# Attention and a maxout layer on one core: where AV, masks and loads of the first batch stand

## The chip, the core and the metric

The kernel runs on one core of a Trainium2 chip. A core has five engines that run their own instruction streams and wait for each other by semaphores: PE (matrix multiply, with PEld for its weight loads), DVE (vector), ACT (scalar functions), POOL (GpSimd) and SP (which only issues transfers here). SP's transfers of q and k and the outputs are queue q1 of the profile, POOL's transfers, which also change fp32 to bf16 on the way, are queue q0. The metric is the device time of one execution in microseconds.

## The reference

There are 8 batches of 8 heads, 576 tokens, head size 64. Attention is causal by blocks of 64 tokens; its output goes, token by token, through a layer of two products and a maximum.

```python
scores = scale * np.matmul(q, k.transpose(0, 1, 3, 2))
mask = block_i >= block_j                     # block = 64 tokens
scores = np.where(mask, scores, -1000000000.0)
scores = scores - np.max(scores, axis=-1, keepdims=True)
attn = np.exp(scores)
attn = attn / (np.sum(attn, axis=-1, keepdims=True) + 1e-09)
attn_out = np.matmul(attn, v)
x = attn_out.transpose(0, 2, 1, 3).reshape(B * S, H * D)
g = np.maximum(x @ w1, x @ w2)
out = g @ w_out
```

## The kernel before

**The algebra.** max(x w1, x w2) is max(x (w1 - w2), 0) + x w2. So the kernel forms d = w1 - w2 on DVE (`diff_w`), M = w2 w_out on PE, and then out = relu(x d) w_out + x M. M needs w2 transposed: `bT_unit` transposes a quarter of w2 (8 transposes), `m_unit` makes an eighth of M (8 matmuls). `h_unit` makes one of 8 slices of relu(x d) for 512 tokens (4 matmuls), `y_unit` 128 rows of the output (12 matmuls).

**Pairs and groups.** Heads are worked on in pairs: pair p holds two heads in the two halves of the partitions, four pairs are a batch, and two pairs are a group, whose q (and whose k) comes in one transfer of 576 KB. There are 16 groups. For each group q and k are cast to bf16, transposed on PE (`transposes`, L362) and copied to qT and kT (L370). Scores are made with keys as rows, ACT takes their exp into aT (L405), and the part of a diagonal block that a query may not see is set to zero (`mask`, L410). `av` (L496) multiplies aT with v, whose extra column of ones gives the softmax sum, and DVE divides (L502, L503). `x_out` transposes the result to xT (L534 to L540); when the last group of a batch is through, its tokens are free for h and y.

**Batch 0 in bursts.** For pairs 0 to 3 the scores of a pair are packed in four pieces, `burst_p` (queries below 256), `burst_q1`, `burst_q2` and `burst_q3`, with one exp each (768, 1024, 1024 and 384 columns over both heads). The pieces go through two PSUM buffers (`ps_s`), so a burst waits for the exp two bursts before it; some have one or two warm-up matmuls ahead of them (L416). AV of a pair is called in two parts: `av(p, [0, 1])` for queries below 256, which needs only the first piece, its masks and two of the five parts of v (6 matmuls), and `av(p, [2, 3, 4])` for the rest (24 matmuls). Everything else on PE takes turns in four PSUM buffers (`ps_m`).

**The order.** No scheduler moves anything: each engine works in the order in which the Python code calls its instructions. `fill(n)` puts n matmuls' worth of the units above in a place, taken from a fixed list whose head is four `bT_unit`s (2 each in this count) and eight `m_unit`s (4 each). POOL's order is also the gate for loads: `load_qk(g, ..., gated=True)` has POOL write one column of the target, and SP's transfer waits for that; v, w1, w2 and w_out are issued by POOL itself. A transfer that POOL issues also waits until the eighth transfer before it, which has the same semaphore, is through. From group 2 on, scores go in regions of 1024-column tiles (`tile_0` to `tile_2`); the loop over groups from the fourth on is the same in both kernels.

**Where v comes in.** v of a batch comes in five parts of 128 tokens (the last of 64), in pieces of 64 elements per head and token. Those of batch 1 are requested behind w1 and group 3: three of them at once, two behind the copies of kz (L388), which wait for kT of group 2.

Of the kernel before, what the change touches and what calls it, by code (L numbers as in the profile page):

```python
# [14 lines left out]
def kernel(  # L15
# [10 lines left out]
    nc = tc.nc  # L26
# [27 lines left out]
    NCH = 5  # L54
# [50 lines left out]
    dve, pool, act = nc.vector.tensor_copy, nc.gpsimd.tensor_copy, nc.scalar.copy  # L105

    def load_qk(g, queues, gated=False):
        b, u = divmod(g, GPB)
        for nm, src, queue in (("q", q, queues[0]), ("k", k, queues[1])):
            if queue is None or by_dma(nm, g):  # L110
                continue
            raws[nm, g] = t = raw.tile([P, 2, RPP * D], FP32, name=f"{nm}raw")
            if gated:
                nc.gpsimd.memset(t[:, 0, :1], 0.0)
            queue.dma_start(
                out=t[:],
                in_=src[b, 4 * u:4 * u + 4].rearrange(
                    "(s h) (p t) d -> (h p) s (t d)", h=2, t=RPP),
            )
# [27 lines left out]
    def cast(nm, g, parts):  # L147
        if by_dma(nm, g):
            return
        t = raws[nm, g].rearrange("p s (t d) -> p t s d", d=D)  # L150
        if (nm, g) not in qk_n:
            qk_n[nm, g] = qkn.tile([P, RPP, 2, D], BF16, name=f"{nm}n")
        n = qk_n[nm, g]
        for copy, j0, j1 in parts:
            copy(out=n[:, j0:j1], in_=t[:, j0:j1])  # L155
# [19 lines left out]
    def load_w1(j):  # L175
        w1_raw[j] = wraw.tile([P, NDM, WB], FP32, name="w1raw")
        nc.gpsimd.dma_start(out=w1_raw[j][:], in_=w1r[:, :, j * WB:(j + 1) * WB])
# [14 lines left out]
    dve, pool, act = nc.vector.tensor_copy, nc.gpsimd.tensor_copy, nc.scalar.copy  # L192
    SP, ACT = nc.sync, nc.scalar
# [138 lines left out]
    def fill(n):  # L332
        while n > 0:
            if not current:
                k = next((k for k, t in enumerate(todo) if t[2] <= done_tokens[0]), None)
                if k is None:
                    return max(0, n)
                current.append(todo.pop(k))
            t = current[0]
            next(t[1])  # L340
            n -= t[3]
            t[0] -= 1
            if not t[0]:
                current.pop()
        return 0
# [76 lines left out]
    def burst_p(p, warm=0):  # L422
        burst(p, ((0, 0, QCUT), (1, P, QCUT - P)), 0, warm)

    def burst_q1(p, warm=0):
        burst(p, ((0, QCUT, 320), (1, QCUT, 192)), 384, warm)

    def burst_q2(p, warm=0):
        burst(p, ((1, 448, P), (2, QCUT, 320), (4, 512, BLK)), 896, warm)

    def burst_q3(p, warm=0):
        burst(p, ((3, 384, 192),), 1408, warm)

    def masks_p(p, eng=None):
        for a in (0, 256):
            mask(p, a, eng)

    def masks_q(p, eng=None):
        for a in (1024, 1408):
            mask(p, a, eng)  # L440
# [39 lines left out]
    def av(p, ts):  # L480
        b, hp = divmod(p, HP)
        vv = vv_r[b % NV]
        a = aT_r[p % NA]
        n = len(ts)
        h0 = hp // 2 * 4 + hp % 2
        if p % 2 == 0 and ts[0] == 0:
            xps[p // 2] = xpool.tile([P, 2, NCH, 2, D], BF16, name="xp")
        xp = xps[p // 2]
        po = ps_m.tile([P, n, 2, D + 1], FP32, name="ps_o", tag="m")
        n_mm = 2 * sum(t + 1 for t in ts)  # L490
        mm = 0
        for gi, t in enumerate(ts):
            for hh in range(2):
                for c in range(t + 1):
                    a0 = a_col(p, c, t)
                    nc.tensor.matmul(  # L496
                        po[:, gi, hh, :], a[:, hh, a0:a0 + P], vv[:, c, h0 + 2 * hh, :],
                        start=(mm == 0), stop=(mm == n_mm - 1),
                    )
                    mm += 1  # L500
        rec = small.tile([P, 3, 2, 1], FP32, name="rec")
        nc.vector.reciprocal(rec[:, :n, :, 0], po[:, :, :, D])  # L502
        nc.vector.tensor_mul(  # L503
            xp[:, :, ts[0]:ts[0] + n, p % 2].rearrange("q s t d -> q t s d"), po[:, :, :, :D],
            rec[:, :n].to_broadcast([P, n, 2, D]),
        )
# [13 lines left out]
    def x_out(g, t0=0, t1=NCH, copies=(dve, dve)):  # L520
        b, u = divmod(g, GPB)
        if x_by_dma(g):
            if u == GPB - 1:
                done_tokens[0] = (b + 1) * S
            return
        xp = xps[g]
        n = t1 - t0
        n_odd = min(t1, NCH - 1) - t0
        pe = ps_m.tile([P, 2, n, BLK], BF16, name="ps_xe", tag="m")
        po = ps_m.tile([P, 2, n_odd, BLK], BF16, name="ps_xo", tag="m")  # L530
        for s in range(2):
            for t in range(t0, t1):
                src = xp[:, s, t].rearrange("p a d -> p (a d)")
                nc.tensor.transpose(pe[:, s, t - t0, :], src[:BLK], ident[:BLK, :BLK])  # L534
                if t < NCH - 1:
                    nc.tensor.transpose(po[:, s, t - t0, :], src[BLK:], ident[BLK:, BLK:])
        dst = xT[:, 2 * u:2 * u + 2, b * S + t0 * P:b * S + t1 * P].rearrange(
            "p s (t h w) -> p s t h w", h=2, w=BLK)
        copies[0](out=dst[:, :, :, 0], in_=pe[:])
        copies[1](out=dst[:, :, :n_odd, 1], in_=po[:])  # L540
        if u == GPB - 1:
            done_tokens[0] = min(b * S + t1 * P, (b + 1) * S)
# [54 lines left out]
    cast("k", 1, ((dve, 0, RPP),))  # L597
    burst_p(0)
    burst_p(1)
    masks_p(0, nc.vector)  # L600
    warm_up(2)
    burst_q1(0)
    burst_q2(0, 2)
    tq = transposes("q", 1, (dve, dve))
    burst_q3(0, 1)
    tk = transposes("k", 1, (dve, dve))
    tq((0,))
    tk((0,))
    tq((1,))
    masks_q(0, nc.vector)  # L610
    tk((1,))
    masks_p(1, nc.vector)
    fill(2)
    burst_q1(1)
    av(0, [0, 1])
    burst_q2(1)
    fill(2)
    av(0, [2, 3, 4])
    burst_q3(1, 1)
    masks_q(1)  # L620
    av(1, [0, 1])
    burst_p(2)
    burst_p(3, 1)
    masks_p(2)
    masks_p(3)
    av(1, [2, 3, 4])
    burst_q1(2)
    x_out(0)
    fill(2)
    burst_q2(2)  # L630
    mask(2, 1024)
    load_qk(2, (SP, None), gated=True)
    av(2, [0, 1])
    burst_q3(2)
    mask(2, 1408)
    fill(2)
    burst_q1(3)
    av(3, [0, 1])
    fill(4)
    burst_q2(3)  # L640
    mask(3, 1024)
    load_qk(2, (None, SP), gated=True)
    av(2, [2, 3, 4])
    fill(4)
    burst_q3(3)
    mask(3, 1408)
    load_w1(0)
    load_w1(1)
    cast("q", 2, ((pool, 0, RPP),))
    load_qk(3, (SP, None), gated=True)  # L650
    load_w1(2)
# [3 lines left out]
        load_v(1, c)  # L655
    fill(8)
    av(3, [2, 3, 4])
    fill(4)
    x_out(1, 0, NCH, (act, dve))
    transposes("q", 2, (dve, act))()  # L660
    cast("k", 2, ((act, 0, RPP),))
    fill(8)
# [118 lines left out]
```

## Time and profile before

| | us |
|---|---|
| median of 13 runs | 262.97 |
| lowest and highest run | 260.39 and 266.12 |
| the profiled execution | 264.97 |
| its span, first to last instruction | 263.2 |
| busy in the span: PE, DVE, ACT, POOL | 248.7, 151.1, 120.3, 120.8 |
| mean granted TensorE clock | 0.984 |

The profile is of one execution. The page gives busy time over the whole span; stretches, waits and the order in time come from queries of the same trace. In a row of the timeline stand the start, the duration of the merged group, the engine, the line, the operation, what it writes and reads, the count, and in brackets the idle time before it with what ended it. In the merged chain a row has start, duration, engine and tile. In a list of waits a row has the waiting engine, what it waited for, the time in all, the count and the longest.

### The profile page before, as it was taken

What the parts mean: (1) busy time and instruction counts of PE and PEld (TensorE: products, weight loads), DVE (VectorE), ACT (ScalarE), POOL (GpSimd) and SP (SyncE); (2) the same over time, 40 slices, a digit from 0 to 9 for tenths busy, and PEclk for the clock granted to TensorE, in tenths of its full rate; (3) what the DMA queues carried; (4) which work ended last, traced back from release to release, by engine and by line L of the source; (5) the groups of instructions that cost most, each with busy time, mean ns of one, the idle gap of its engine ahead of it and who ended that gap; (6) DMA issues with size and microseconds to landing.
All of it is one profiled execution on the core that took longest, in us unless ns stands there. A gap on an engine that the chain in (4) does not pass through costs nothing.

```text
span 263.2 us, 6742 instructions
## 1 busy us (share of the span) xinstructions
PE 248.7 (94%) x2765; PEld 134.7 (51%) x2765; DVE 151.1 (57%) x308; ACT 120.3 (46%) x158; POOL 120.8 (46%) x282
## 2 busy tenths in 40 slices
PE   8869988599999999999999999999999999999994
PEld 3436853255555546464646455555555555444443
DVE  5975578536658537662775376538643764664521
ACT  2746288345765664655546463737363500000000
POOL 2931495517886865857384739374530100000000
PEclk9997999979999999999999999999999999999998
DMA  7999699928999999999999999999973212202122
GB/s 252 230 162 129 213 332 261 255 73 71 226 195 127 200 158 255 191 183 174 184 239 126 202 189 158 194 186 196 132 97 103 67 27 81 80 2 80 48 110 82
DMA packets 104383, 41.27 MB, mean 157 GB/s; under 512 B 89248, under 2 KB 93728, under 8 KB 104352
## 3 DMA queue, kind: packets, MB, share of 16 engines
q0 software_dynamic: 65952, 11.87, 58.9%
q1 hardware_dynamic: 37984, 28.32, 47.9%
q10 hardware_dynamic: 416, 0.66, 0.7%
q8 instruction: 21, 0.34, 0.6%
q14 instruction: 10, 0.08, 0.1%
HBM read 34.60 MB, written 9.44 MB: 167 GB/s over the span
## 4 chain that ended last, share of the span: by engine, by line
PE 84%; DMA 10%; POOL 2%; ACT 1%; DVE 1%; issue 0%
PE ps_y L273 36%; PE ps_h L231 21%; PE ps_o L496 11%; DMA vv<-in_v_dram 8%; PE ps_s L381 8%; PE ps_M L254 3%; PE ps_qT L362 2%; DMA qraw<-in_q_dram 2%; POOL vv L159 1%; PE ps_y L288 1%; PE ps_s L399 1%; POOL xT L180 1%; PE ps_xe L534 1%; PE ps_kT L362 0%; ACT aT L405 0%; POOL kz L388 0%
## 5 line engine op out<-in xcount | busy, mean ns | idle before, releaser
L405 ACT ACTIVATE aT<-ps_s 128x1024 bf16<-128x1024 f32 (+2 forms) x100 | 96.0, 994 | 50.9 <-PE ps_s L381 39.4
L273 PE MATMUL ps_y<-wo_sb,g 128*128 128x512 bf16 x280 | 71.4, 380 | 0.0
L231 PE MATMUL ps_h<-xT,d_sb 128*128 128x512 bf16 x288 | 68.2, 380 | 0.2 <-DVE d_sb L183 0.2
L236 DVE TENSOR_SCALAR g<-ps_h 128x512 bf16<-128x512 f32 x72 | 49.6, 690 | 18.3 <-PE ps_h L231 18.3
L410 POOL MEMSET aT<- 64x128 bf16 x122 | 21.8, 199 | 76.9 <-ACT aT L405 76.2
L278 DVE COPY y<-ps_y 128x512 f32<-128x512 f32 x35 | 24.2, 691 | 46.2 <-PE ps_y L273 45.6
L496 PEld LDWEIGHTS <-aT 128*128 128x128 bf16 x960 | 38.5, 99 | 20.1 <-issue 6.2
L496 PE MATMUL ps_o<-vv,aT 128*128 128x65 bf16 x960 | 41.8, 195 | 4.9 <-DMA vv<-in_v_dram 4.7
L231 PEld LDWEIGHTS <-d_sb 128*128 128x128 bf16 x288 | 26.4, 98 | 31.4 <-issue 2.9
L273 PEld LDWEIGHTS <-g 128*128 128x128 bf16 x280 | 24.9, 98 | 30.5 <-issue 6.2
L273 PE MATMUL ps_y<-m_sb,xT 128*128 128x512 bf16 x140 | 38.4, 385 | 0.0
L381 PE MATMUL ps_s<-qT,kT 64*128 64x128 bf16 (+6 forms) x344 | 32.1, 286 | 2.7 <-ACT kT L370 1.5
L159 POOL DMA_DIRECT2D vv<-in_v_dram x40 | 33.9, 859 | 0.9 <-issue 0.5
L503 DVE TENSOR_TENSOR xp<-ps_o,rec 128x256 bf16<-128x256 f32 (+1 forms) x64 | 31.4, 491 | 2.2
L502 DVE RECIPROCAL rec<-ps_o 128x4 f32<-128x4 f32 (+1 forms) x64 | 12.0, 187 | 32.8 <-PE ps_o L496 32.4
L132 POOL DMA_DIRECT2D kb<-in_k_dram x40 | 29.4, 760 | 0.0
L293 ACT COPY y<-ps_y 128x256 f32<-128x256 f32 (+1 forms) x2 | 0.6, 318 | 49.3 <-PE ps_y L288 49.3
L370 ACT COPY qT<-ps_qT 128x576 bf16<-128x576 bf16 x15 | 9.6, 639 | 27.0 <-PE ps_qT L362 25.6
L273 PEld LDWEIGHTS <-xT 128*128 128x128 bf16 x140 | 12.9, 98 | 14.4 <-issue 1.2
L155 POOL CAST qn<-qraw 128x1152 bf16<-128x1152 f32 (+1 forms) x15 | 16.5, 1100 | 5.7 <-DMA qraw<-in_q_dram 5.6
L381 PEld LDWEIGHTS <-kT 64*128 64x128 bf16 x344 | 11.9, 95 | 13.9 <-issue 7.1
L370 DVE COPY qT<-ps_qT 128x576 bf16<-128x576 bf16 x17 | 12.7, 749 | 0.4 <-PE ps_qT L362 0.2
(58 smaller groups left out, 138.0 us busy)
## 6 DMA issues: line engine op xcount, KB each, us to landing
qraw<-in_q_dram SPq DMA_DIRECT2D x16, 576.0 KB, 5.0
out_dram<-y SPq DMA_DIRECT2D x35, 256.0 KB, 4.0
vv<-in_v_dram POOLq DMA_DIRECT2D x32, 128.0 KB, 6.3
kraw<-in_k_dram SPq DMA_DIRECT2D x5, 576.0 KB, 7.4
kb<-in_k_dram POOLq DMA_DIRECT2D x40, 72.0 KB, 6.6
w1raw<-in_moe_w_dram POOLq DMA_DIRECT2D x4, 512.0 KB, 6.5
xT<-in_moe_w_dram POOLq DMA_DIRECT2D x4, 256.0 KB, 6.0
wo_sb<-in_moe_w_out_dram POOLq DMA_DIRECT2D x2, 512.0 KB, 10.2
```

The lines of the kernel that those rows point to most:

```text
L132: nc.gpsimd.dma_start(out=n[h * BLK:(h + 1) * BLK, :, s], in_=(q if nm == "q" else k)[b, 4 * u + 2 * s + h].rearrange("(j p) d -> p j d", ...
L159: nc.gpsimd.dma_start(out=vv_r[b % NV][P - rows:, c, :, :D], in_=v[b, :, c * P:c * P + rows, :].rearrange("h p d -> p h d"),)
L231: nc.tensor.matmul(pt[:], d_sb[:, c, f * P:(f + 1) * P], xT[:, c, t0:t0 + SPAN], start=(c == 0), stop=(c == NDM - 1),)
L236: nc.vector.tensor_scalar_max(g[:, f], pt[:], 0.0)
L273: nc.tensor.matmul(py[:], lhs, rhs, start=(n == 0), stop=(n == len(terms) - 1),)
L278: nc.vector.tensor_copy(out=y[:], in_=py[:])
L370: (copy or copies[i])(out=t[:, p0 * RPP:p1 * RPP].rearrange("q (p j) -> q p j", j=RPP), in_=pts[i][:, :, p0:p1].rearrange("q j p -> q p j"),)
L381: nc.tensor.matmul(ps[:, hh, col:col + w], kT[r, k0:k0 + P], qT[r, q0:q0 + w], start=True, stop=True,)
L405: nc.scalar.activation(out=aT_r[p % NA][:, :, a0:a0 + w], in_=ps[:, :, :w], func=AF.Exp, scale=scale,)
L410: (eng or nc.gpsimd).memset(aT_r[p % NA][BLK:, :, a0:a0 + BLK], 0.0)
L496: nc.tensor.matmul(po[:, gi, hh, :], a[:, hh, a0:a0 + P], vv[:, c, h0 + 2 * hh, :], start=(mm == 0), stop=(mm == n_mm - 1),)
L503: nc.vector.tensor_mul(xp[:, :, ts[0]:ts[0] + n, p % 2].rearrange("q s t d -> q t s d"), po[:, :, :, :D], rec[:, :n].to_broadcast([P, n, 2 ...
```

## The change

Four things are changed in the code that orders the work of batch 0 and the loads behind it. The early AV parts of pairs 0 and 1 move from among the bursts of pairs 1 and 2 to behind `burst_q1(2)`, their late parts to behind `burst_q3(2)` and `burst_q1(3)`, and `x_out(0)` to behind `burst_q3(3)`. The masks of pairs 0 and 1, six of which DVE wrote, are all written by POOL, behind its last request for w_out. The gated loads of q and k of group 2 and the first two quarters of w1 move ahead in POOL's order. Units of `fill` change places with them: two `fill(2)` stand ahead of the bursts of pairs 1 to 3, and `fill(8)` stands on both sides of the late AV part of pair 3.

```diff
     burst_p(0)
     burst_p(1)
-    masks_p(0, nc.vector)
     warm_up(2)
     burst_q1(0)
     burst_q2(0, 2)
     tq = transposes("q", 1, (dve, dve))
     burst_q3(0, 1)
     tk = transposes("k", 1, (dve, dve))
-    tq((0,))
-    tk((0,))
-    tq((1,))
-    masks_q(0, nc.vector)
-    tk((1,))
-    masks_p(1, nc.vector)
+    for i in range(2):
+        tq((i,))
+        tk((i,))
+    burst_q1(1)
     fill(2)
-    burst_q1(1)
-    av(0, [0, 1])
     burst_q2(1)
+    burst_q3(1, 1)
+    for p in range(2):
+        masks_p(p)
+    for p in range(2):
+        masks_q(p)
+    burst_p(2, 1)
     fill(2)
-    av(0, [2, 3, 4])
-    burst_q3(1, 1)
-    masks_q(1)
-    av(1, [0, 1])
-    burst_p(2)
     burst_p(3, 1)
     masks_p(2)
     masks_p(3)
-    av(1, [2, 3, 4])
     burst_q1(2)
-    x_out(0)
-    fill(2)
+    av(0, [0, 1])
+    av(1, [0, 1])
     burst_q2(2)
     mask(2, 1024)
-    load_qk(2, (SP, None), gated=True)
     av(2, [0, 1])
     burst_q3(2)
     mask(2, 1408)
-    fill(2)
+    load_qk(2, (SP, None), gated=True)
+    av(0, [2, 3, 4])
     burst_q1(3)
-    av(3, [0, 1])
-    fill(4)
+    load_qk(2, (None, SP), gated=True)
+    av(1, [2, 3, 4])
     burst_q2(3)
     mask(3, 1024)
-    load_qk(2, (None, SP), gated=True)
+    load_w1(0)
+    fill(2)
     av(2, [2, 3, 4])
-    fill(4)
     burst_q3(3)
     mask(3, 1408)
-    load_w1(0)
     load_w1(1)
+    fill(2)
+    x_out(0)
+    av(3, [0, 1])
     cast("q", 2, ((pool, 0, RPP),))
     load_qk(3, (SP, None), gated=True)
     load_w1(2)
@@
         load_v(1, c)
     fill(8)
     av(3, [2, 3, 4])
+    fill(8)
+    x_out(1, 0, NCH, (act, dve))
     fill(4)
-    x_out(1, 0, NCH, (act, dve))
     transposes("q", 2, (dve, act))()
```

The first place is POOL behind its requests for w_out; aT_107 and aT_108 are the aT tiles of pairs 2 and 3, qraw and kraw the targets of group 2. This is the difference (- before, + the change):

```order
 L410 MEMSET aT_108 64x2x64 x2
-L410 MEMSET aT_107 64x2x64
+L410 MEMSET aT_107 64x2x64 x2
 L114 MEMSET qraw 128x1
-L410 MEMSET aT_107 64x2x64
-L410 MEMSET aT_108 64x2x64
 L114 MEMSET kraw 128x1
 L410 MEMSET aT_108 64x2x64
-L177 DMA w1raw<-in_moe_w_dram 128x4x256 x2
+L177 DMA w1raw<-in_moe_w_dram 128x4x256
+L410 MEMSET aT_108 64x2x64
+L177 DMA w1raw<-in_moe_w_dram 128x4x256
```

The gate of q now stands behind one more mask of pair 2 and the gate of k directly behind it, no longer behind masks of pair 3; the two first requests for w1 stand around pair 3's last mask. Ahead of this piece POOL now also has all eight masks of pairs 0 and 1.

The second place is DVE behind the copies of kT of group 1, which shows where each AV part stands: a reciprocal of 128x4 follows an early part, one of 128x6 a late part, and bT_sb is the copy behind a `bT_unit`. Before, where xp_330 is the result of group 0:

```order
L245 COPY bT_sb_111<-ps_bT_314 128x1024
L502 RECIPROCAL rec_338<-ps_o_331 128x4
L503 TENSOR_TENSOR xp_330<-ps_o_331,rec_338 128x2x2x64
L245 COPY bT_sb_111<-ps_bT_349 128x1024
L502 RECIPROCAL rec_384<-ps_o_359 128x6
L503 TENSOR_TENSOR xp_330<-ps_o_359,rec_384 128x3x2x64
L502 RECIPROCAL rec_401<-ps_o_394 128x4
L503 TENSOR_TENSOR xp_330<-ps_o_394,rec_401 128x2x2x64
L502 RECIPROCAL rec_446<-ps_o_421 128x6
L503 TENSOR_TENSOR xp_330<-ps_o_421,rec_446 128x3x2x64
L539 COPY xT_109<-ps_xe_455 128x2x5x64
```

In the change, where xp_379 is that of group 0 and xp_409 that of group 1:

```order
L245 COPY bT_sb_111<-ps_bT_314 128x1024
L245 COPY bT_sb_111<-ps_bT_352 128x1024
L502 RECIPROCAL rec_387<-ps_o_380 128x4
L503 TENSOR_TENSOR xp_379<-ps_o_380,rec_387 128x2x2x64
L502 RECIPROCAL rec_397<-ps_o_390 128x4
L503 TENSOR_TENSOR xp_379<-ps_o_390,rec_397 128x2x2x64
L502 RECIPROCAL rec_417<-ps_o_410 128x4
L503 TENSOR_TENSOR xp_409<-ps_o_410,rec_417 128x2x2x64
L502 RECIPROCAL rec_453<-ps_o_428 128x6
L503 TENSOR_TENSOR xp_379<-ps_o_428,rec_453 128x3x2x64
L502 RECIPROCAL rec_490<-ps_o_465 128x6
L503 TENSOR_TENSOR xp_379<-ps_o_465,rec_490 128x3x2x64
```

Before, early and late parts took turns, pair by pair, with a `bT_unit` between them, and the copy to xT followed pair 1. Now both `bT_unit`s come first, then the early parts of pairs 0, 1 and 2, then the late parts of pairs 0 and 1, and the copy to xT no longer stands among them.

## The prediction

> **What bounds the kernel now.** The cut into stretches comes first, because a share over 263 us hides which stage waits. Its columns: stretch and length, busy time and instructions of PE, PEld, DVE, ACT and POOL, the granted TensorE clock, the DMA share, GB/s.
>
> ```profile
> 12.70:16.10 3.40, 2.51 (x41) 1.74 (x40) 3.17 (x10) 2.10 (x3) 2.56 (x4) 1.00 2.50 138
> 16.10:19.50 3.40, 1.73 (x30) 1.05 (x28) 1.75 (x5) 0.51 (x2) 0.20 (x1) 1.00 1.53 182
> 19.50:22.90 3.40, 3.15 (x39) 1.98 (x37) 1.18 (x4) 1.93 (x4) 0.89 (x5) 0.50 1.46 198
> 24.50:26.50 2.00, 1.91 (x27) 1.46 (x27) 1.85 (x6) 1.90 (x3) 0.50 (x3) 1.00 0.06 9
> 36.60:40.00 3.40, 2.67 (x26) 1.17 (x24) 2.15 (x4) 3.15 (x5) 3.15 (x7) 1.00 1.01 366
> 43.40:46.80 3.40, 2.44 (x26) 0.94 (x26) 3.40 (x6) 2.88 (x5) 1.78 (x5) 1.00 1.58 251
> 50.20:53.60 3.40, 1.71 (x24) 1.12 (x24) 1.21 (x3) 0.00 (x0) 1.47 (x3) 1.00 1.10 307
> 53.60:57.00 3.40, 3.37 (x40) 1.76 (x38) 1.42 (x3) 2.06 (x4) 0.35 (x2) 0.50 0.11 39
> 57.00:263.20 206.20, 202.17 (x2155) 107.34 (x2153) 113.68 (x227) 88.24 (x115) 91.87 (x216) 1.00 1.07 139
> ```
>
> After 57 us PE works 202.17 of 206.20 us, so the rest of the program is a fixed block of PE work: whatever the first 57 us give up moves the end by as much. Two things are lost there. Twice the clock is halved for 3.4 us, each time right behind a stretch in which PE was busy for about half (1.73 and 1.71 of 3.40); stretches with 2.51 and 2.44 were not followed by that. At half speed 3.4 us do the work of 1.7.
>
> The Trainium skill (TensorE: Matmul & The Clock Gate, Part 1) says that the gate is judged in free-running windows of 3.4 us, and in its closing table that gaps up to about 3 us between bursts are safe. The length agrees with 19.50 to 22.90; the safe gap does not, since no single wait for v was longer than 1.5 us. By the closing table the clock term below would be nil and the sum 258.7.
>
> The other loss is waiting. The list of PE's waits up to 60 us, then pieces of PE's order in time:
>
> ```profile
> PE ps_o L496 <- DMA vv<-in_v_dram: 4.7, 5, 1.5
> ```
>
> ```profile
> 17.68 0.91 PE L496 MATMUL ps_o<-vv,aT 128*128 128x65 bf16 x15 [1.54 <-DMA vv<-in_v_dram]
> ...
> 37.34 0.61 PE L381 MATMUL ps_s<-qT,kT 64*128 64x512 bf16 x6 [0.73 <-ACT kT L370]
> ...
> 49.30 0.26 PE L496 MATMUL ps_o<-vv,aT 128*128 128x65 bf16 x3
> ...
> 53.22 0.95 PE L496 MATMUL ps_o<-vv,aT 128*128 128x65 bf16 x15 [0.74 <-DMA vv<-in_v_dram]
> 54.11 0.66 PE L362 MATMUL ps_qT<-ident,qn 64*128 64x64 bf16 x18
> ...
> 57.59 0.35 PE L496 MATMUL ps_o<-vv,aT 128*128 128x65 bf16 x6
> ...
> 59.26 0.44 PE L362 MATMUL ps_kT<-ident,kn 64*128 64x64 bf16 x18
> ```
>
> AV of pair 4 needs the values of batch 1, which come last. From 49.30 to 54.11 it takes 4.81 us, while the same sequence for pair 5 (6 AV matmuls, 3 others, 24 AV matmuls) takes 59.26 - 57.59 = 1.67: **3.14 us lost to v**. Why v is late stands on Pool and SP:
>
> ```profile
> 13.42 1.84 POOL L189 DMA_DIRECT2D wo_sb<-in_moe_w_out_dram  x2
> ...
> 30.21 1.53 POOL L177 DMA_DIRECT2D w1raw<-in_moe_w_dram  x2 [0.28 <-issue]
> ...
> 34.42 2.67 POOL L159 DMA_DIRECT2D vv<-in_v_dram  x3
> ...
> 38.37 1.57 POOL L159 DMA_DIRECT2D vv<-in_v_dram  x2
> ```
>
> ```profile
> 25.70 0.37 SPq L115 DMA_DIRECT2D qraw<-in_q_dram  x1
> ...
> 40.07 0.37 SPq L115 DMA_DIRECT2D qraw<-in_q_dram  x1
> ```
>
> Nothing is requested between 15.3 us and q of group 2 at 25.70. From 24.5 to 26.5 the DMA engines move 9 GB/s. What follows is then a queue: w1, q and k of group 3, v, and from 40.07 q and k of group 4.
>
> **The burst stage (first term).** Scores go through two PSUM buffers, so ACT's exp paces the bursts.
>
> ```profile
> 8.85 3.94 ACT L405 ACTIVATE aT<-ps_s 128x768 bf16<-128x768 f32 x5
> ...
> 22.61 1.02 ACT L405 ACTIVATE aT<-ps_s 128x1024 bf16<-128x1024 f32 x1 [1.17 <-PE ps_s L381]
> ...
> 29.12 0.49 ACT L405 ACTIVATE aT<-ps_s 128x384 bf16<-128x384 f32 x1 [0.87 <-PE ps_s L381]
> ```
>
> The first five end at 12.79. Eleven are left: another such five (3.94), four of 1024 (4.08) and two of 384 (0.98), 9.0 us, so 21.8 if ACT never waits. Now the last ends at 29.61, because AV parts that wait for v stand between the bursts (the longest wait, 1.54 us, ends at 17.68) and the clock then drops. In the change AV of pairs 0 and 1 comes after eleven of the sixteen bursts, at about 17 us by this chain, and its later parts near 19, when v of batch 0 has landed (17.68). I add 1.2 us for places where ACT still waits: two warm matmuls and a unit of 8 transposes stand ahead of the bursts of pairs 2 and 3, each behind a buffer that has to come free. The last exp then ends at 23.0, its scores at 22.5. The merged chain gives what PE does next:
>
> ```profile
> 23.31 0.55 PE ps_bT L243 x8
> ...
> 25.70 0.29 PE ps_o L496 x6
> 25.99 0.87 PE ps_M L254 x8
> 26.87 0.33 PE ps_s L381 x6
> 27.19 0.83 PE ps_o L496 x24
> ...
> 28.90 0.19 PE ps_s L381 x2
> ...
> 36.24 0.41 PE ps_kT L362 x18
> ```
>
> Ahead of the first M unit stand one more set of 8 transposes (0.55), the x transposes and 6 AV matmuls (0.29 each, about): 23.6. From the first M unit (25.99) to the end of the k transposes (36.65) PE now needs 10.66 us without a gap; of it 0.33 + 0.83 + 0.19 = 1.35 lies ahead of M in the change, so 9.3 remain. The k transposes end at 32.9, and with the 0.73 until kT is copied, region 4 starts at 33.7 where it now starts at 37.34: 3.6 us earlier. The data for it comes in time: q of group 2 is requested at 20.4 (after the last exp of pair 2, about 20.0, and its mask) instead of 25.70, w1 from 22.5 instead of 30.21, and nothing of them is needed before 29.
>
> **What that request costs.** Packets in one microsecond: queue q1 (q and k) beside q0 (v) at 46 us; q0 alone with v at 12 us; q0 alone with w_out at 22 us; then w_out's first half and the last v, with the us to landing.
>
> ```profile
> q1 hardware_dynamic: 152, 0.32, 92.4%
> q0 software_dynamic: 151, 0.02, 28.7%
> ...
> q0 software_dynamic: 1227, 0.15, 242.5%
> ...
> q0 software_dynamic: 388, 0.20, 145.0%
> ...
> wo_sb<-in_moe_w_out_dram POOLq DMA_DIRECT2D x1, 512.0 KB, 9.3
> ...
> vv<-in_v_dram POOLq DMA_DIRECT2D x1, 64.0 KB, 14.4
> ```
>
> With both queues active each gets as many packets as the other, 152 and 151, and q0 drops from 1227. Now w_out's first half lands at 13.42 + 9.3 = 22.7, undisturbed. In the change q of group 2 starts moving near 21.4, and the 1.3 us left of that half take up to 1.3 x 388/151 = 3.3: it lands between 22.7 and 24.7, and the M unit at 23.6 waits 0 to 1.1 us. I take 0.6, the middle. **First term: 3.0** (2.5 to 3.6; 4.8 if ACT never waits).
>
> The Trainium skill (DMA: Bandwidth & Descriptors, "Queues, rings and completion order") has the rule behind this: each engine changes between queues at packet boundaries, so larger packets take the bytes. It speaks against asking for q and k behind w_out, and the trace agrees (152 and 151). It gives rival B.
>
> **The masks.** Six memsets leave DVE, six join Pool.
>
> ```profile
> L410 POOL MEMSET aT<- 64x128 bf16 x122 | 21.8, 199 | 76.9 <-ACT aT L405 76.2
> ```
>
> Pool is through with w_out at 15.26; eight masks at 0.2 us end by 16.9, just ahead of the AV at 17 that needs the first four. Cost nothing; without that cover at most 1 us of AV wait while bursts go on being queued. The other order of the AV parts and of fill units adds no instruction to PE: each unit is only placed elsewhere.
>
> **From region 4 to AV of pair 4 (second term).** PE waits here, but DVE is full (3.40 of 3.40 from 43.4 to 46.8), so earlier loads cannot shorten it much: 0.2 taken, 0 to 1.3.
>
> **v of batch 1 (third term).** q and k of group 2 and the rest of w_out are through by 26. Then w1 (2.1 MB) and group 3 (1.2 MB) at the 366 GB/s of 36.6 to 40.0: 9.0 us, to 35. v's first three parts are requested about 28, the last two behind the kz copies of region 4, 3 us earlier than 38.37, and q of group 4 right after, at 37, moving from 38. From 35 to 38 v has the engines to itself: 3 x 1227 = 3,700 of its 4,608 packets (576 rows of 8 heads). The rest shares with group 4 and lands by 43; AV of pair 4 asks at 49.30 - 3.2 = 46.1. So all 3.1 go, with 3 us to spare. The other end is 0: v lands as long after its request as now (14.4 us), moves by 3 us like PE, and the stall stays. I take 3.1, as the free interval is worked out from rates of this trace.
>
> **The clock (fourth term).** Without the stall the stretch before 53.6 is no longer half empty: 1.7 (0 to 1.7). The first slow stretch lies inside the first term.
>
> Sum: 3.0 + 0.2 + 3.1 + 1.7 = 8.0 against the profiled execution's 264.97 (span 263.2 and 1.8 around it): **257.0**. That execution is 2.0 above the median 262.97; the runs spread from 260.39 to 266.12, which is three half-clock stretches' worth, so I read the median's advantage as fewer slow stretches, not to be gained a second time. 257.0 stands, 6.0 below the median.
>
> **Rivals.** A, v still comes last: if w1 and group 3 need until 38, v shares with group 4 until 42 and meets group 5. For it: v took 14.4 us to land. Against it: 3 us of margin. The third and fourth terms go: 257.0 + 4.8 = 261.8, and a median run about 261. B, w_out is starved and the idle stretch round 24 us (1.1 us of wait beside thin x transposes) halves the clock in the M units: 257.0 + 0.5 + 1.7 = 259.2. C, slower: the clock oscillates. With AV out of the bursts, PE is thin from 12.4 to 16 (4 bursts); each half-clock stretch fills PE, the next is thin again. Place: 12 to 57 us, price 1.7 per stretch; slower from the sixth on: 257.0 + 10.2 = 267.2. Against it: M units are dense and 2.51 of 3.40 was enough. D, the requests do not come earlier since ACT paces the gates no faster; only the AV wait of 1.54 us and what follows it on the clock, at most 1.7, go, half of that hidden behind ACT: 264.97 - 1.6 = 263.4, or about 262 in a median run.
>
> **How the numbers follow.** Forecast 0.58 (own range 254.5 to 258.5), A 0.13, B 0.17, C 0.05, D 0.07. The low end takes ACT without waits (1.8) and DVE's 1.1 as well: 254.1, with a lucky clock 253.3; the high end covers B and most of A: 261.3. Differences of 0.5%, 1.3 us, are about what can be told: faster means under 261.65. Forecast, B and two thirds of A: 0.84 with a little left over for D; same 0.10, slower 0.06.
>
> **What would show it.** The last exp of the bursts near 23; a request for q of group 2 near 20.4; the M unit's wait on w_out under 1.1 us; region 4 near 34; no AV wait for v after 40 us and a clock of 1.00 from there on. The forecast is wrong if v of batch 1 lands after 47, or if the clock shows more than one slow stretch between 12 and 57 us.

## The result, and the profile after

| | before | after |
|---|---|---|
| median of the runs beside each other, us | 263.09 (48 runs) | 256.95 (11 runs) |
| lowest and highest, us | 260.39 and 266.53 | 256.39 and 258.22 |
| the profiled execution, us | 264.97 | 257.51 |
| its span, us | 263.2 | 255.7 |
| mean granted TensorE clock in it | 0.984 | 1.00 |

The ratio of the changed kernel to the one before is **0.979 (95% interval 0.976 to 0.981)**; ratios here and below leave out the runs that lie more than 1.5% above the fastest of their kernel. Predicted were 257.0 us. The gain is clear of the noise; whether it is over 2% the interval leaves open.

First the cut into stretches of the changed kernel, with the columns of the prediction's first rows (stretch and length, busy time of PE, PEld, DVE, ACT and POOL, granted clock, DMA share, GB/s):

```profile
12.70:16.10 3.40, 2.77 (x33) 1.49 (x33) 2.68 (x4) 2.94 (x5) 3.36 (x10) 1.00 2.46 143
16.10:19.50 3.40, 2.99 (x61) 2.19 (x59) 2.33 (x7) 3.17 (x5) 1.10 (x7) 1.00 1.55 185
19.50:22.90 3.40, 3.40 (x82) 2.78 (x79) 2.49 (x7) 2.61 (x5) 0.74 (x5) 1.00 1.45 197
...
43.30:46.70 3.40, 2.29 (x20) 1.14 (x21) 2.33 (x5) 1.80 (x2) 2.10 (x9) 1.00 0.49 175
46.70:50.10 3.40, 3.40 (x63) 2.11 (x62) 2.56 (x7) 1.75 (x4) 1.73 (x5) 1.00 0.90 291
...
57.00:255.70 198.70, 194.62 (x2026) 102.48 (x2021) 109.95 (x218) 84.68 (x110) 87.53 (x206) 1.00 1.10 143
```

The two half-clock stretches are gone: where PE was busy for 1.73 of 3.40 us it is now for 2.99, and where it was for 1.71 for 3.40. The emptiest stretch between 12.7 and 50 us is now 43.3 to 46.7 with 2.29, and the clock stays at 1.00 behind it.

PE's order in time at the places that the prediction named (the first M units; the start of region 4; two waits; AV of pair 4 in two parts; the q transposes behind it):

```profile
24.05 1.91 PE L254 MATMUL ps_M<-wo_sb,bT_sb 128*128 128x256 bf16 x16
...
34.01 0.61 PE L381 MATMUL ps_s<-qT,kT 64*128 64x512 bf16 x6 [0.73 <-ACT kT L370]
...
40.74 1.04 PE L231 MATMUL ps_h<-xT,d_sb 128*128 128x512 bf16 x4 [0.99 <-DVE d_sb L183]
...
44.41 0.61 PE L381 MATMUL ps_s<-qT,kT 64*128 64x512 bf16 x6 [1.29 <-DVE kT L370]
...
46.25 0.34 PE L496 MATMUL ps_o<-vv,aT 128*128 128x65 bf16 x6
...
47.08 0.89 PE L496 MATMUL ps_o<-vv,aT 128*128 128x65 bf16 x24
47.90 0.44 PE L362 MATMUL ps_qT<-ident,qn 64*128 64x64 bf16 x18
```

From these rows and the prediction's, piece by piece: region 4 starts at 34.01, 3.33 earlier than 37.34. From there to AV of pair 4 it takes 46.25 - 34.01 = 12.24, before 49.30 - 37.34 = 11.96: 0.28 lost. AV of pair 4 takes 47.90 - 46.25 = 1.65, before 4.81: 3.16 gained. From 47.90 to the end of the span it is 207.8, before 263.2 - 54.11 = 209.1: 1.3 gained. The sum, 3.33 - 0.28 + 3.16 + 1.3 = 7.5, is the difference of the spans.

The requests of SP and the last exp of the bursts on ACT:

```profile
20.37 0.37 SPq L115 DMA_DIRECT2D qraw<-in_q_dram  x1
20.78 0.47 SPq L115 DMA_DIRECT2D kraw<-in_k_dram  x1
```

```profile
22.76 0.49 ACT L405 ACTIVATE aT<-ps_s 128x384 bf16<-128x384 f32 x1 [0.44 <-PE ps_s L381]
```

The last exp ends at 23.25, q of group 2 is requested at 20.37. The packets in the microseconds from 22, from 23 and from 24 show when that request began to move:

```profile
q0 software_dynamic: 390, 0.20, 146.0%
...
q0 software_dynamic: 241, 0.12, 87.5%
q1 hardware_dynamic: 64, 0.15, 38.2%
...
q1 hardware_dynamic: 166, 0.37, 96.6%
q0 software_dynamic: 27, 0.01, 11.4%
```

From 22 to 23 only q0 moves, with 390 packets; q1 begins in the microsecond behind it. So q starts almost 3 us after its request, just as the first half of w_out is through.

### The profile page after: what moved, and what is told of

Read it like the earlier page. It is cut to its first block, busy times and chain, and to the rows that moved or that the text cites. A ratio compares the mean times of both kernels' runs of the same rounds, so it can differ in the third digit from the quotient of the medians.

```text
span 255.7 us, 6744 instructions
## 1 busy us (share of the span) xinstructions
PE 245.1 (96%) x2766; PEld 133.0 (52%) x2766; DVE 150.3 (59%) x302; ACT 120.0 (47%) x158; POOL 120.8 (47%) x288
## 4 chain that ended last, share of the span: by engine, by line
PE 91%; ACT 3%; DVE 3%; issue 1%
PE ps_y L273 37%; PE ps_h L231 24%; PE ps_o L496 11%; PE ps_s L381 9%; PE ps_M L254 3%; PE ps_w L351 2%; ACT aT L405 2%; PE ps_qT L362 2%; PE ps_y L288 1%; PE ps_s L399 1%; DVE d_sb L183 1%; PE ps_kT L362 1%; DVE g L236 1%; ACT kT L370 0%; PE ps_s L416 0%
## 5 line engine op out<-in xcount | busy, mean ns | idle before, releaser
L410 POOL MEMSET aT<- 64x128 bf16 x128 | 22.6, 199 | 63.7 <-ACT aT L405 63.0
L496 PEld LDWEIGHTS <-aT 128*128 128x128 bf16 x960 | 37.3, 98 | 14.0 <-issue 0.4
L496 PE MATMUL ps_o<-vv,aT 128*128 128x65 bf16 x960 | 39.6, 194 | 0.0
L273 PE MATMUL ps_y<-m_sb,xT 128*128 128x512 bf16 x140 | 37.8, 379 | 0.0
L381 PE MATMUL ps_s<-qT,kT 64*128 64x128 bf16 (+6 forms) x344 | 31.2, 280 | 3.4 <-ACT kT L370 1.5
L370 ACT COPY qT<-ps_qT 128x576 bf16<-128x576 bf16 x15 | 9.6, 639 | 24.0 <-PE ps_qT L362 22.6
L370 DVE COPY qT<-ps_qT 128x576 bf16<-128x576 bf16 x17 | 12.7, 749 | 0.7 <-PE ps_qT L362 0.7
## 6 DMA issues: line engine op xcount, KB each, us to landing
out_dram<-y SPq DMA_DIRECT2D x35, 256.0 KB, 3.9
xT<-in_moe_w_dram POOLq DMA_DIRECT2D x4, 256.0 KB, 6.0
```

Source lines behind the costliest of these rows:

```text
L273: nc.tensor.matmul(py[:], lhs, rhs, start=(n == 0), stop=(n == len(terms) - 1),)
L370: (copy or copies[i])(out=t[:, p0 * RPP:p1 * RPP].rearrange("q (p j) -> q p j", j=RPP), in_=pts[i][:, :, p0:p1].rearrange("q j p -> q p j"),)
L381: nc.tensor.matmul(ps[:, hh, col:col + w], kT[r, k0:k0 + P], qT[r, q0:q0 + w], start=True, stop=True,)
L410: (eng or nc.gpsimd).memset(aT_r[p % NA][BLK:, :, a0:a0 + BLK], 0.0)
L496: nc.tensor.matmul(po[:, gi, hh, :], a[:, hh, a0:a0 + P], vv[:, c, h0 + 2 * hh, :], start=(mm == 0), stop=(mm == n_mm - 1),)
```

## The experiments

**Loads alone.** The kernel before, with the requests moved ahead and the order of PE left as it was.

```diff
     masks_p(2)
+    load_qk(2, (SP, SP), gated=True)
     masks_p(3)
+    load_w1(0)
+    load_w1(1)
     av(1, [2, 3, 4])
@@
     mask(2, 1024)
-    load_qk(2, (SP, None), gated=True)
@@
     mask(3, 1024)
-    load_qk(2, (None, SP), gated=True)
@@
     mask(3, 1408)
-    load_w1(0)
-    load_w1(1)
```

> The kernel before, with only the requests moved: q and k of group 2 behind the masks of pair 2 and the first two quarters of w1 behind those of pair 3, so near 21 and 22 us, as in the change. AV, bursts, masks and fill stay. Theory (v of batch 1 is late because of the queue ahead of it, and the DMA gap is what is wasted): bursts and region 4 stay where they are (37.3 us), the slow clock behind the AV waits for batch 0 stays, but v of batch 1 lands near 43, the 3.1 us of AV wait at 49 us and the slow clock behind it go: 258.5 us. Rival (the order of AV carries the gain, requests follow by themselves): 262.5 to 263. Rival (the requests carry all): 257.

Measured 260.97 (260.38 to 261.32), ratio 0.991 (0.988 to 0.994): some 2.4 us of the change's gain, less than expected. AV of pair 4 takes 1.65 us here as well, so the loads alone remove the second wait and the second slow stretch. The first slow stretch stays. In this execution the clock is halved from 15.6 to 22.4, 6.8 us and not the 3.4 of the profile before, though the edit changes nothing ahead of that; so region 4 starts at 38.32, 1.0 later than before. q of group 2 is requested at 22.40, 2.0 later than in the change. The cut:

```profile
16.10:19.50 3.40, 2.15 (x28) 1.58 (x25) 0.99 (x3) 0.46 (x1) 0.20 (x1) 0.50 1.71 176
19.50:22.90 3.40, 3.40 (x42) 1.86 (x41) 1.27 (x4) 2.12 (x3) 0.70 (x6) 0.57 1.45 197
```

**Order alone.** The changed kernel, with the gates of q and k of group 2 (here written by DVE) and the requests for w1 put back to about the times of before.

```diff
     mask(2, 1408)
-    load_qk(2, (SP, None), gated=True)
     av(0, [2, 3, 4])
     burst_q1(3)
-    load_qk(2, (None, SP), gated=True)
@@
-    load_w1(0)
     fill(2)
@@
-    load_w1(1)
     fill(2)
@@
     av(3, [0, 1])
+    fill(4)
+    load_qk(2, (SP, None), gated=True, geng=nc.vector)
+    fill(4)
+    av(3, [2, 3, 4])
+    fill(8)
+    load_qk(2, (None, SP), gated=True, geng=nc.vector)
     cast("q", 2, ((pool, 0, RPP),))
+    load_w1(0)
+    load_w1(1)
     load_qk(3, (SP, None), gated=True)
@@
         load_v(1, c)
-    fill(8)
-    av(3, [2, 3, 4])
-    fill(8)
     x_out(1, 0, NCH, (act, dve))
```

> The change, with its order of AV, bursts, masks and fill, but the requests held back to about where the kernel before makes them: q of group 2 gated near 25.7 us and k near 28.7 (by a column that DVE writes between copies of M), w1 from 30 on. Theory: the last exp of the bursts still ends near 23 and the clock is full there, but region 4 waits for w1 (first h unit not before 36) and v of batch 1 lands near 53 as before, so AV of pair 4 waits longer and ends where it did: 261.5 to 263. Rival (the order of AV alone carries the gain): 257 to 259.

Measured 262.60 (261.47 to 264.59), ratio 1.000 (0.997 to 1.004), as expected: nothing. PE comes to the M units at 23.6 us, but then stands for data:

```profile
30.50 0.44 PE L362 MATMUL ps_qT<-ident,qn 64*128 64x64 bf16 x18 [1.12 <-POOL qn L155]
...
42.67 0.51 PE L362 MATMUL ps_qT<-ident,qn 64*128 64x64 bf16 x18 [2.09 <-POOL qn L155]
```

Behind the second of these waits the clock is halved as well, from 42.9 to 46.3, and AV of pair 4 still waits 0.76 us for v. So loads alone are worth 0.9%, order alone nothing, both 2.1%. Order without loads moves the wait to Pool's casts, which wait for q; loads without order leave the first thin stretch and the half clock behind it.

**q and k of group 2 asked for at once.** In the changed kernel their gates stand right behind the requests for w_out.

```diff
     burst_q3(1, 1)
+    load_qk(2, (SP, SP), gated=True)
     for p in range(2):
         masks_p(p)
@@
     mask(2, 1408)
-    load_qk(2, (SP, None), gated=True)
     av(0, [2, 3, 4])
     burst_q1(3)
-    load_qk(2, (None, SP), gated=True)
```

> The change, with both gates of group 2 moved ahead of all masks, right behind the requests for w_out (about 15.4 us instead of 20.4). Theory of the prediction (both queues send packet for packet): q and k move from 16.5 on, w_out falls from 390 to 150 packets per us, its first half lands near 26 and the M units wait 2 to 3 us: 259 to 260. Rival (what was requested first is served first, since in the changed kernel q of group 2 began to move only at 23 us, behind w_out): q and k move from 23 on again, M does not wait, 257.0.

Measured 260.44 (258.18 to 262.60), ratio 0.988 (0.984 to 0.993): sharing by packets, as my theory had it, and some 3 us worse than the changed kernel. The requests go out at 15.33 and 15.75; the first packets move at 19, 3.7 us later. The packets in the microsecond from 20, then a row of PE's waits up to 60 us, then the cut:

```profile
q1 hardware_dynamic: 111, 0.26, 73.5%
q0 software_dynamic: 117, 0.06, 43.2%
```

```profile
PE ps_M L254 <- DMA wo_sb<-in_moe_w_out_dram: 2.6, 1, 2.6
```

```profile
22.90:26.30 3.40, 1.31 (x32) 1.03 (x32) 2.34 (x6) 0.30 (x1) 3.36 (x7) 1.00 1.38 228
26.30:29.70 3.40, 2.31 (x11) 1.64 (x12) 0.39 (x1) 0.00 (x0) 3.30 (x5) 0.50 1.12 355
```

This is the prediction's rival B in the flesh: q and k take every second packet, the M units wait 2.6 us for w_out, the stretch before 26.3 is thin and the clock is halved behind it, from 26.3 to 33.1. Two of the ten runs kept the clock at 0.999 or more and still took 258.2 and 258.6, some 1.4 us over the changed kernel. The change escapes this by asking 5 us later.

**Masks back on DVE.** In the changed kernel DVE writes the six masks of before.

```diff
     burst_p(1)
+    masks_p(0, nc.vector)
     warm_up(2)
@@
-    for i in range(2):
-        tq((i,))
-        tk((i,))
+    tq((0,))
+    tk((0,))
+    tq((1,))
+    masks_q(0, nc.vector)
+    tk((1,))
+    masks_p(1, nc.vector)
@@
-    for p in range(2):
-        masks_p(p)
-    for p in range(2):
-        masks_q(p)
+    masks_q(1)
```

> The change, with the six masks of pairs 0 and 1 on DVE where they were before. Theory (the masks cost nothing on either engine): 257.0, within 0.5. Rival (masks between the copies of qT and kT hold back the scores of pair 2): the burst of pair 2 starts 0.3 to 0.6 us later, 257.5.

Measured 256.89 (256.67 to 257.07), ratio 0.976 (0.973 to 0.979): the masks are worth nothing, on either engine.

**Filling the waits.** The kernel before, with 6 and 9 matmuls of zeros ahead of the two AV parts that wait for v; they add work and change nothing that is computed.

```diff
     def av_with(p, n):
+        if p == 4:
+            warm_up(9)
         av(p, [0, 1])
@@
     fill(2)
+    warm_up(6)
     av(0, [2, 3, 4])
```

> The kernel before, with matmuls on zeros put into its two long waits for v and nothing taken away: 6 ahead of the late AV part of pair 0 (1.3 us, into the wait that ends at 17.7) and 9 ahead of AV of pair 4 (1.9 us, into the waits of 49 to 53). Theory (the clock is halved behind a stretch of 3.4 us in which PE was busy for about half): both slow stretches go, the mean granted clock rises from 0.987 to 0.997 or more, the waits for v stay, and 263.1 falls by 1.3 to 2.7: 260.4 to 261.8. Rival (the clock falls for another reason, or single gaps decide): clock 0.987 and 263 or a little more.

Measured 262.58 (260.83 to 264.47), ratio 1.005 (1.001 to 1.008), where 260.4 to 261.8 were expected. The time is a miss, the mechanism is not. The cut and PE's order:

```profile
16.10:19.50 3.40, 2.90 (x41) 1.72 (x40) 1.64 (x6) 0.61 (x2) 0.20 (x1) 1.00 1.63 182
19.50:22.90 3.40, 2.88 (x65) 2.08 (x65) 1.73 (x5) 2.54 (x3) 0.89 (x5) 1.00 1.46 198
```

```profile
48.81 2.10 PE L351 MATMUL ps_w<-zeros 128*128 128x512 bf16 x9
...
50.75 0.34 PE L496 MATMUL ps_o<-vv,aT 128*128 128x65 bf16 x6
```

With the wait filled PE is busy for 2.90 of 3.40 and the clock stays whole (mean 0.997 or more in seven of ten runs, against four of nineteen of the kernel before beside them). So the half clock does come from the thin stretch before it. But the fillers occupy PE for 1.94 us in front of AV of pair 4. Those seven runs have a median of 262.3, the four of the kernel before with the same clock 261.0: the fillers cost about 1.3 us, as much as the clock gives. About 0.9 us between 52.4 us and the end is in no wait that I found.

**v early.** The kernel before, with all of v of batch 1 requested right behind w_out.

```diff
     load_wo(1)
+    for c in range(NCH):
+        load_v(1, c)
@@
-    for c in range(3):
-        load_v(1, c)
@@
-    load_v(1, 3)
-    load_v(1, 4)
     load_qk(4, (SP, SP), gated=True)
```

> The kernel before, with v of batch 1 requested directly behind w_out (from 15.3 us) and the rest where it was. Theory (v comes last only because of the queue ahead of it): it lands near 29, the AV waits at 49 us (3.1) and the slow clock behind them (1.3) go, bursts and their slow clock stay: 258.7. Rival (the DMA is full anyway, so w1 or group 3 is late in place of v): 262 to 263.

Measured 261.49 (260.58 to 262.39), ratio 0.997 (0.994 to 1.001): not 258.7. AV of pair 4 takes 1.65 us, so that wait is gone; but whatever goes ahead of the queue pushes something else back. Pool now stands for q of groups 2 and 3, in the list of its waits up to 60 us:

```profile
POOL qn L155 <- DMA qraw<-in_q_dram: 7.9, 2, 4.5
```

PE's waits for qT and d rise from 0.2 us each to 0.8 and 0.6; that for kT is 0.9 as before. And the first stretch at half clock is still there, in this execution for 6.8 us, from 16.9 to 23.7:

```profile
16.10:19.50 3.40, 2.17 (x29) 1.42 (x25) 1.76 (x6) 0.57 (x1) 2.46 (x4) 0.62 1.57 188
19.50:22.90 3.40, 3.40 (x43) 2.10 (x43) 0.88 (x3) 2.11 (x3) 2.17 (x8) 0.50 1.45 198
```

AV of pair 4 starts at 50.47, 1.2 later than before. The rival, that w1 or group 3 come late instead, was nearer.

**v late.** The changed kernel with one thing undone: the last two parts of v of batch 1 are requested at 47.2 us.

```diff
     pad_keys(5)
-    load_v(1, 3)
-    load_v(1, 4)
     load_qk(4, (SP, SP), gated=True)
@@
     cast("q", 4, ((pool, 0, RPP),))
+    load_v(1, 3)
+    load_v(1, 4)
     cast("k", 4, ((pool, 0, RPP),))
```

> The changed kernel with one thing undone: the last two parts of v of batch 1 are requested behind Pool's cast of q of group 4 (about 47 us) instead of at 34.8. They should land about 50.5, so the late part of AV of pair 4, which asks at 47.1, waits about 3.4 us. My theory: this costs the wait and, if PE falls to about half of a 3.4 us stretch, one stretch at half clock (1.2): 257.0 + 3.4 + 1.2 = 261.6 (260.5 to 262.5), the granted clock near 0.99. Rival, the wait alone is paid and the clock stays at 1.00: 260.4. Rival, PE makes good part of it later, since other engines run ahead meanwhile: under 259.5.

Measured 265.86 (265.48 to 267.13), ratio 1.015 (1.011 to 1.019); the changed kernel in the same group 257.16 (256.89 to 257.90). One late load makes the kernel slower than the one before. PE's order and the cut:

```profile
53.62 1.01 PE L496 MATMUL ps_o<-vv,aT 128*128 128x65 bf16 x15 [5.79 <-DMA vv<-in_v_dram]
```

```profile
49.40:52.80 3.40, 0.00 (x0) 0.00 (x0) 0.00 (x0) 0.00 (x0) 0.89 (x3) 0.70 1.48 290
52.80:56.20 3.40, 2.58 (x44) 1.83 (x44) 1.42 (x3) 0.86 (x2) 0.00 (x0) 0.50 0.04 6
56.20:59.60 3.40, 3.40 (x37) 1.78 (x36) 0.61 (x2) 2.01 (x3) 1.17 (x4) 0.79 0.00 0
```

The mechanism is as expected, the size is not: v came 6.3 us after its request, and PE waited 5.79 instead of 3.4. It did not share with q and k of group 5: from the request at 47.24 until 50.8 only q1 moved, and then v came at 700 to 860 packets per microsecond. AV of pair 4 takes 54.56 - 46.56 = 8.0 instead of 1.65 (6.35 more), the rest of the program 209.1 instead of 207.7 (1.4 more; the clock is halved from 50.8 to 57.6), and 0.6 comes from ahead of AV: 8.4, the difference of the spans (263.7 and 255.3). Nothing is made good later.

**All loads before the cast.** The changed kernel, with the last two quarters of w1 and q and k of group 3 requested ahead of Pool's cast of q of group 2.

```diff
     av(3, [0, 1])
-    cast("q", 2, ((pool, 0, RPP),))
-    load_qk(3, (SP, None), gated=True)
     load_w1(2)
     load_w1(3)
-    load_qk(3, (None, SP), gated=True)
+    load_qk(3, (SP, SP), gated=True)
+    cast("q", 2, ((pool, 0, RPP),))
```

> The change, with the other two quarters of w1 and q and k of group 3 requested ahead of POOL's cast of q of group 2 (from 24.6 us, not 28.6), since POOL waits there 2.9 us for q. Theory (in the change PE's waits of 1.0 for d and 1.3 for kT between 40 and 44 us come from DVE's difference for the third quarter, which took 2.05 us beside POOL's cast of k of group 3): k lands earlier, the cast is over before 38.6, the difference takes 1.2 to 1.4 and PE waits 0.6 to 0.8 less: 256.2. Rival (DVE's chain is as long as before): 257.0.

Measured 257.85 (256.99 to 258.69), ratio 0.985 (0.979 to 0.991); no gain, where 256.2 was expected. The third difference for d took 1.26 us and PE's wait for it 0.42, as expected, but a new wait is longer than what was won:

```profile
PE ps_M L254 <- DMA wo_sb<-in_moe_w_out_dram: 1.8, 1, 1.8
```

**The differences earlier as well.** On top of the last, `diff_w(2)` and `diff_w(3)` stand right behind the first tiles of region 4.

```diff
     region(tile_0(4), tile_1(4), masked=False)
-    fill(8)
-    region(tile_2(4), tile_0(5), masked=False)
-    masks(4)
-    fill(4)
     diff_w(2)
     fill(4)
+    diff_w(3)
+    fill(4)
+    region(tile_2(4), tile_0(5), masked=False)
+    masks(4)
+    fill(8)
     copy_out = transposes("q", 3, (dve, act))
@@
     copy_out()
-    diff_w(3)
     region(*outs, masked=False)
```

> As more_loads, and DVE takes the differences for the third and fourth quarter of w1 right behind the first tiles of region 4 (34 to 36.5 us, where DVE is idle for 1.7 us in the change) and not between the copies of qT and kT of group 3. Theory (DVE's chain is what holds PE from 40 to 44 us): both waits go but for some 0.3: 254.8 to 255.2. Rival (the copies of relu move back and PE waits for its buffers instead, or w1 is not there yet): 256.2 or more.

Measured 255.81 (255.46 to 256.18), ratio 0.978 (0.974 to 0.982). Both of DVE's waits are gone, and region 4 to AV of pair 4 takes 10.0 us instead of 12.24. The time is still above the 254.8 to 255.2 expected; 0.6 us of it is a new wait for the cast of q of group 4. To compare directly, it ran once more beside the changed kernel, with a variant that moves only w1 ahead of the cast and has the two differences early too:

> The changed kernel once more, so that the others of this group stand beside it. Expected 256.9 (256.4 to 258.2), the ratio to the kernel before 0.979.

> The changed kernel with the last w1 and group 3 requested ahead of Pool's cast of q of group 2, and with the last two differences for d right behind the first tiles of region 4. My theory: what is left on the way from region 4 to the first AV of batch 1 is 0.99 us of waiting for d and 1.29 us for kT, both behind DVE's late differences; without them, and with 0.6 us of a new wait for q of group 4, 255.3 to 256.0, some 1.2 below the changed kernel beside it. Rival, the earlier 255.81 was a quicker chip: then no difference to the changed kernel of this group, within 0.5 us.

```diff
     av(3, [0, 1])
-    cast("q", 2, ((pool, 0, RPP),))
-    load_qk(3, (SP, None), gated=True)
     load_w1(2)
     load_w1(3)
+    cast("q", 2, ((pool, 0, RPP),))
+    load_qk(3, (SP, None), gated=True)
     load_qk(3, (None, SP), gated=True)
```

> As the one before, but only the last two quarters of w1 go ahead of the cast; q and k of group 3 stay behind it. They travel in a queue of their own that shares packet for packet with w_out, while w1 stands in w_out's queue behind it. My theory: early w1 is what the differences need, so the time is that of the one before, 255.3 to 256.0, without the risk of a wait for the second half of w_out. Rival, the request of group 3 is what counts (k of group 3 was cast 0.89 us late in the changed kernel): then 256.3 to 257.

Measured: the changed kernel 257.16 (256.89 to 257.90), with all loads and differences early 256.98 (255.77 to 257.89), with w1 and differences early 256.28 (255.38 to 256.61). The ratios to the kernel before are 0.982 (0.978 to 0.986), 0.980 (0.975 to 0.985) and 0.978 (0.974 to 0.981). All six runs of the last lie below all six of the changed kernel, by 0.9 us in the median, so it is the best of this group, though the intervals of the ratios overlap; it lies between what its theory (255.3 to 256.0) and its rival (256.3 to 257) said. The middle one misses its expectation of 255.3 to 256.0: it lies 0.2 us below the changed kernel, within the 0.5 that its rival allowed. It has three runs between 255.77 and 256.65 and three between 257.31 and 257.89, one of which is the profiled one. Its order in time, DVE and POOL:

```profile
36.28 3.91 DVE L183 TENSOR_TENSOR d_sb<-w1raw,xT 128x1024 bf16<-128x1024 f32 x1 [0.25 <-DMA w1raw<-in_moe_w_dram]
...
36.86 1.16 POOL L155 CAST qn<-qraw 128x1152 bf16<-128x1152 f32 x1
...
37.95 1.16 POOL L155 CAST kn<-kraw 128x1152 bf16<-128x1152 f32 x1
```

and of the variant with w1 and differences early:

```profile
36.92 1.23 DVE L183 TENSOR_TENSOR d_sb<-w1raw,xT 128x1024 bf16<-128x1024 f32 x1 [0.18 <-DMA w1raw<-in_moe_w_dram]
...
37.66 1.49 POOL L155 CAST qn<-qraw 128x1152 bf16<-128x1152 f32 x1
```

In the first DVE's difference takes 3.91 us, until both casts of Pool are through (37.95 + 1.16 = 39.11) and 1.08 more, and PE waits 2.15 us behind it. In the second it takes its 1.23 us, and Pool's cast is the one that is stretched. The next section says what this has to do with the prediction.

## Why the prediction was right, and where not

**The first term (3.0, own bounds 2.5 to 3.6): measured 3.33.** The last exp at 23.25 (23.0 predicted), the request for q at 20.37 (20.4), region 4 at 34.01 (about 34.3). This trace starts its first burst 0.29 us later than that of before (9.14 against 8.85), so the true gain is 3.6, the upper bound. The step that failed is the 0.6 for the wait of the M units on w_out: there is none. The prediction let q begin 1 us after its request, as it does in the kernel before (requested at 25.70 into idle engines). Behind a busy queue it began after almost 3 us, when w_out's first half was through (22.6). The other half of the step was right: once q moves, the queues go packet for packet, as the request at 15.33 shows (111 and 117).

**The second term (0.2 gained, 0 to 1.3): measured 0.28 lost.** This step was wrong, also in its bounds, which left out a loss. It read DVE as full and stopped there. The earlier loads did take away PE's waits for the casts of q and k of group 3 (0.20 and 0.62 us in the kernel before), but PE's waits for DVE grew by more: from 0.17 to 0.99 for d and from 0.94 to 1.29 for kT. The rows of DVE and POOL in the kernel before, which the prediction did not set side by side, say more:

```profile
41.18 1.14 POOL L155 CAST qn<-qraw 128x1152 bf16<-128x1152 f32 x1 [1.10 <-DMA qraw<-in_q_dram]
41.96 1.44 DVE L183 TENSOR_TENSOR d_sb<-w1raw,xT 128x1024 bf16<-128x1024 f32 x1
...
43.91 1.15 POOL L155 CAST kn<-kraw 128x1152 bf16<-128x1152 f32 x1 [1.59 <-DMA kraw<-in_k_dram]
44.60 1.54 DVE L183 TENSOR_TENSOR d_sb<-w1raw,xT 128x1024 bf16<-128x1024 f32 x1
```

and in the changed one:

```profile
38.47 1.15 POOL L155 CAST kn<-kraw 128x1152 bf16<-128x1152 f32 x1 [0.89 <-DMA kraw<-in_k_dram]
38.64 2.05 DVE L183 TENSOR_TENSOR d_sb<-w1raw,xT 128x1024 bf16<-128x1024 f32 x1
```

By these rows a difference that starts while a cast runs does nothing until the cast ends, and then takes 1.07 or 1.08 us: 42.32 + 1.08 = 43.40, 45.06 + 1.08 = 46.14, 39.62 + 1.07 = 40.69. So the time of such an instruction depends on the tenth of a microsecond at which it starts. The change moved the third difference from 0.78 us behind the start of a cast to 0.17 behind it, which cost 0.6 us. PE's wait of 0.99 us for d is this (0.17 before). Its wait of 1.29 for kT stands behind the fourth difference: it stayed where the third was quick (1.26 us, all loads before the cast) and went where both were early. In the kernel with the order alone it is the other way round:

```profile
40.39 1.22 DVE L183 TENSOR_TENSOR d_sb<-w1raw,xT 128x1024 bf16<-128x1024 f32 x1
...
40.83 1.79 POOL L155 CAST qn<-qraw 128x1152 bf16<-128x1152 f32 x1 [2.53 <-DMA qraw<-in_q_dram]
```

The difference starts first, the cast waits until 41.61 and needs 1.01 more. The Trainium skill (SBUF — State Buffer, "SBUF: two separate sides") states this rule: DVE with two inputs from SBUF and a GpSimd instruction that reads SBUF share a pair of ports under an exclusive lock, whoever starts first keeps it for the whole instruction, and the other blocks. All of these rows agree. One does not: the difference of 3.91 us began 0.58 ahead of the cast and still lost; it began while Pool was issuing transfers for v, but so did the one at 36.92, which was not held. That stays open.

**The third term (3.1): measured 3.16.** No AV part waits for v after 40 us. v was requested at 30.1 and 34.8 and moved alone at about 1,200 packets per microsecond from 37 to 40. Moving its last two parts back brings a wait for v (5.8 us), so its arrival was the term's cause. Rival A, v late again, did not occur, but the margin was not the 3 us of the prediction, which had v there by 43. From 42 to 46 q0 still moved about 10 packets per microsecond, and the last part of v, requested at 35.7, took this many us to land (the last number):

```profile
vv<-in_v_dram POOLq DMA_DIRECT2D x1, 64.0 KB, 11.1
```

That is 46.7 to 46.8, and the late part of AV starts at 47.08: only about 1 us was to spare. In the variant with w1 and differences early, where this AV part starts at 45.28, PE does wait 0.30 us for v. Why the last packets came so slowly is not shown.

**The fourth term (1.7): measured 1.3.** The rule was right; the size was too large because part of the price was counted twice. The halved stretch begins at 53.6, 0.5 us ahead of 54.11, and slows the last 15 matmuls of AV of pair 4. They take 54.11 - 53.22 = 0.89 us there, but 52.25 - 51.70 = 0.55 at full clock in the kernel with the order alone:

```profile
51.70 0.61 PE L496 MATMUL ps_o<-vv,aT 128*128 128x65 bf16 x15 [0.76 <-DMA vv<-in_v_dram]
52.25 0.44 PE L362 MATMUL ps_qT<-ident,qn 64*128 64x64 bf16 x18
```

These 0.34 us stand in the third term already; with the 1.3 they make 1.6, nearly the 1.7 of the prediction. In the runs of the kernel before that stood beside the experiments, the mean clock tells how many such stretches there were (each lowers it by 0.0065): none in 9 runs, median 260.97; one in 20, 261.88; two in 17, 263.78. That is 0.9 for the first and 1.9 for the second, 1.4 on average; what else differs between these runs is not recorded. The same runs bear out the reading that the median lies below the profiled execution by fewer slow stretches, but only in part: with two of them, like the middle of its kind, that execution would have taken 263.8, not 264.97; the other 1.2 us are not explained.

**The sum.** 7.5 of span against 8.0 predicted: 3.33 for 3.0, -0.28 for 0.2, 3.16 for 3.1, 1.3 for 1.7. The misses have both signs. That the median of 256.95 meets 257.0 so closely is luck: the sum was made for the profiled execution, which took 257.51, and the terms were off by up to 0.5 us. Rivals C and D fell with the clock at 1.00 and the request at 20.37. B's w_out wait came about in kernels that ask earlier: 2.6 us with q and k at 15.33, the half clock behind it, and about 3 us lost; 1.8 us with all loads before the cast.

What the parts are worth one by one does not add up to the whole: loads 2.4 us, order and masks nothing, together 5.6 by the ratio. My reading is that each takes away one of two things that wait for each other, and that the prediction's sum came out because it followed the path with both in place; the runs of the loads alone have a mean clock of 0.985 to 0.991, no better than before, and those of the change one of 0.997 to 1.00.

## What to carry to other kernels

Cut the span into stretches before costing anything: where the end is a full block of one engine's work, only what happens before it counts, and it counts in full. Test an earlier load for what it shares the engines with, and an earlier order for whether its data is there; each alone can be worth nothing. Set the rows of DVE and Pool side by side wherever DVE reads two operands from SBUF: an instruction that takes half as long again in some places may have waited for the other engine, and a shift of some tenths of a microsecond can decide it.

## What the runs showed of the hardware that was not expected

- **The start of a transfer behind a busy queue.** q on SP's queue began to move about 1 us after its request on idle engines (25.70), but 2.9 us (20.37) and 3.7 us (15.33) after it while Pool's queue was full. In the other direction, v (request at 47.24) began 3.6 us after it, behind q and k. What holds it is not shown.
- **The clock.** Where it changes between 5 and 70 us of these traces it goes to 0.50 and comes back after 3.4 or 6.8 us; the four changes in the kernel before (19.5, 22.9, 53.6, 57.0) lie multiples of 3.4 us apart. In the 3.4 us ahead of each halving PE was busy for at most 1.97 us: 1.73 and 1.71 in the kernel before, 1.97 with the loads alone (12.2 to 15.6), 1.91 with v early (13.5 to 16.9), 1.31 with the order alone and with q and k at once. Single waits were at most 1.5 us in the kernel before. The stretch from 46.8 to 50.2 there, with 2.10, was not followed by a halving, so in these traces the limit lies between 1.97 and 2.10 of 3.4 us of busy time as the profile gives it. To come back takes more: the clock rose behind halved stretches in which PE was busy for 3.14 to 3.40 us and stayed down behind those with 0.58 (v late), 2.15 (loads alone), 2.31 (q and k at once) and 2.80 (v early). The Trainium skill (TensorE: Matmul & The Clock Gate, closing table) asks only that gaps stay below about 3 us; these runs do not agree, while its window of 3.4 us fits.
- **The ports of DVE and Pool.** A 128x1024 difference takes 1.21 to 1.23 us alone, and 1.44 to 2.20 us where a cast on Pool still had 0.36 us or more to run when it started (3.91 in the one row that does not fit); a cast of 1.14 us takes up to 2.16 behind a difference.
